# Eleven products of zeros in TensorE's first waits, and a new order of all commands: attention with sinks feeding a three-way maxout layer

## The chip, the core and the metric

The kernel runs on one core of a Trainium2 chip. The metric is the time of one execution on the device in microseconds (us). The kernel before was run five times; the figure that counts is the median. One more execution was taken by the hardware profiler, and all rows of the profile come from it.

## What is computed

Inputs are `q`, `k`, `v` of shape 4 batches x 8 heads x 768 positions x 64, in float32. Three heads (0, 2, 6) attend causally to everything; the five others see only the first 4 positions (the sinks) and a window of 64. The attention output, laid out as 3072 x 512, goes through three projections to 768, their elementwise maximum, and a projection back.

```python
def _attn_ref(q, k, v, is_retrieval, n_sink, window):
    scores = scale * np.matmul(q, k.transpose(0, 1, 3, 2))
    ...
    stream_keep = causal & (is_sink | in_win)
    ...
    scores = np.where(mask[None, :, :, :], scores, -1000000000.0)
    a = np.exp(scores - np.max(scores, axis=-1, keepdims=True))
    a = a / (np.sum(a, axis=-1, keepdims=True) + 1e-09)
    return np.matmul(a, v)

def _moe_ref(x, w1, w2, w3, w_out):
    h = np.maximum(np.maximum(x @ w1, x @ w2), x @ w3)
    return h @ w_out
```

## The kernel before, in words

The work is cut into 16 attention steps and 8 pieces of the feed-forward layer. A step `t` is a batch (`t // 4`), a half of the 384 + 384 query positions, and a quarter set `qd` of the heads (`t % 2`); each step has two pairs of heads, `i` = 0 and 1. A piece of the layer is one batch and one half: 384 tokens.

The order is written out by hand, as a long list of commands called `PROGRAM`. Each command issues a few instructions, and every engine executes its own instructions strictly in the order in which the commands name them. The program is one arm of a branch; the other arm (`GENERAL`) serves other head patterns and does not run here. Before the branch stand the first loads, the masks' raw material and `idle_work(IDLE)`, eight 512-wide products of zeros on TensorE that depend on nothing but a memset.

The commands, with the lines their instructions have in the profile:

- `ld`, `load`, `load_v`, `load_vp`, `w`: DMA loads. `ld`, `load`, `load_vp` and `w` are issued by POOL and stand in POOL's own order; `load_v` by the SP queue. `w 0` to `w 3` are the four weights.
- `cast h p xy` (L314): two casts to fp16, for a pair of heads of batch 0, keys `kn` on engine x and queries `qn` on engine y (d = DVE, a = ACT, p = POOL).
- `turnp` (L333, L341): six TensorE transposes of such a pair, and one or two copies out of PSUM into `KQ`. `turn` (L388): the same for the later batches, by DVE's own 32x32 transpose, 1.1 us each, eight for each batch.
- `um` (L533): a mask built on DVE. For the first two steps masks are added on TensorE (L722, an identity times `mk`).
- `s t u` (L737, L748): scores of one unit on TensorE and their exponential on ACT. The scores go to a pool of two double banks, tag `st`.
- `k t i u e` (L762, L782, L797): masks multiplied into the exponentials, on DVE or POOL.
- `v` (L656, L660, L665, L672): values cast to fp16 into `va`, and copies for the window into `vf`. `o` (L378): sink columns copied in `KQ`.
- `av t i` (L823, L831, L834): the product with the values, then on DVE a reciprocal and a multiplication into `x`.
- `x t i e` (L853, L854, or a DMA transpose L847 with `D`): the transposed input of the layer. The last `x` of a half queues its piece of the layer.
- `f 1 e` (L591, L608, L611, L627, L633): one step of the oldest piece queued: four 384-wide products and their evacuation, or six products of the last projection. A first product's copy goes to engine e; the two maxima are DVE's whatever e says. 24 steps make a piece, 192 in all.
- `idle n`: n more products of zeros; the command exists before the change, but `PROGRAM` does not use it.
- `gate`, `pad`: tiny DMAs that hold the SP queue until something is ready.

```python
    def idle_work(n):
        sink = sps.tile([P, 2, 512], FP32, tag="st", name="st")
        for _ in range(n):
            nc.tensor.matmul(sink[:, 0, :], zero[:, 0:P], zero, start=True, stop=True)
```

In PSUM there are the two `st` tiles and a pool of four single banks (`bkp`, tag `bank`) that everything else shares: the layer's outputs `yy`, the value products `oacc`, the transposes `tr`, and the single-bank scores of `s ... b`. TensorE can therefore run ahead of DVE and ACT by four banks at most.

Of the kernel before, what the change touches and what calls it, by code (L numbers as in the profile page):

```python
# [129 lines left out]
)  # L130

PROGRAM = (
    "cast 0 0 ad, load_v 0 0, cast 0 1 pp, ld 1 0, um 1 1, turnp 0 1 aa, um 1 0, cast 0 3 pa",
    "um 0 1, s 0 0 1, s 0 1 1 b, turnp 0 3 a, cast 0 2 pp, ld 1 2, turnp 0 0 ad, turnp 0 2 ad",
    "um 0 0, cast 1 1 dd, s 0 0 0, cast 1 0 dd, w 0, s 1 0 0, s 0 1 0 b, load_vp 0 1, o 0 0 0 p",
    "v 0 1 dd, v 1 1 dd, v 0 0 dp, turnp 1 0 d, turnp 1 1 da, s 1 0 1, av 0 0, w 1, av 0 1",
    "o 0 1 0 p, cast 1 2 pa, s 1 1 1, s 1 1 0 b, s 2 0 1, v 1 0 pp, cast 1 3 ap, av 1 1",
    "s 2 0 0, av 1 0, x 1 0 d, x 0 0 a, turnp 1 2 dd, s 2 1, x 0 1 d, w 2, x 1 1 d, turnp 1 3 d",
    "f 1 d, s 3 0, k 2 0 1 d, f 1 d, k 3 0 0 d, w 3, o 0 0 1 p, s 3 1 0, k 3 1 0 d, f 1 a",
    "f 1 d, o 0 1 1 d, k 2 1 1 d, s 2 2, v 3 0 dp, f 1 d, k 3 0 1 d, load 1 0, f 1 d, k 2 0 2 d",  # L140
    "v 2 1 dd, s 2 3, av 3 0, s 3 1 1, f 1 a, f 1 d, f 1 d, k 2 1 3 p, v 3 1 ap, k 2 0 3 d",
# [12 lines left out]
    "f 1 d, f 1 a, f 1 a, av 6 1, k 5 1 1 p, s 8 0, f 1 d, av 7 0, load_v 2 0, f 1 a, load 3 1",
    "pad, k 6 0 3 d, av 7 1, s 9 0, x 6 1 D, f 1 d, f 1 d, v 9 1 pp, f 1 a, v 9 0 dp, f 1 a",
    "v 8 1 dd, s 9 1, f 1 a, turn 3 1 1 1, av 6 0, load 3 0, o 2 0 0 d, x 6 0 D, turn 3 1 0 0",
    "f 1 a, x 7 0 D, x 7 1 D, s 8 1, f 1 a, f 1 d, s 10 0, o 2 1 0 p, f 1 d, k 8 0 1 d, f 1 a",
    "turn 3 1 1 0, load_v 2 1, s 9 2, k 9 0 2 d, k 9 1 2 d, f 1 a, f 1 a, v 8 0 ap, f 1 d",
    "f 1 a, k 8 0 0 p, k 9 0 0 d, turn 3 1 0 1, v 10 0 pd, v 11 1 pp, f 1 d, f 1 a, load_v 3 0",
    "f 1 d, f 1 d, f 1 a, k 8 1 0 d, k 9 1 0 d, s 10 1, av 9 0, f 1 a, av 8 0, f 1 a, f 1 a",  # L160
    "v 11 0 pd, f 1 d, f 1 d, k 8 1 1 d, f 1 a, v 12 0 dp, k 9 1 1 p, s 10 2, x 8 0 D, av 9 1",
    "f 1 d, f 1 a, f 1 a, s 10 3, turn 3 0 0 0, av 8 1, x 9 0 D, f 1 a, f 1 d, x 8 1 D, f 1 a",
    "f 1 d, k 10 0 1 p, f 1 d, turn 3 0 0 1, x 9 1 D, k 10 0 3 d, k 10 0 2 d, turn 3 0 1 0",
    "f 1 a, f 1 d, f 1 d, load_v 3 1, f 1 a, k 9 0 1 d, av 10 0, f 1 a, k 10 1 3 p, f 1 d",
    "f 1 d, v 12 1 pp, f 1 a, turn 3 0 1 1, av 11 0, k 10 1 1 p, f 1 d, f 1 a, f 1 a, s 13 0",
# [791 lines left out]
```

## Time and profile before

| | us |
|---|---|
| median of 5 runs | 193.39 (193.27 to 193.82) |
| the profiled execution's own time | 193.64 |
| its span in the trace | 191.9 |
| TensorE busy (products) | 179.8, 94% |
| DVE busy | 145.5, 76% |
| ACT busy | 98.5, 51% |
| POOL busy | 66.8, 35% |
| HBM read / written | 25.17 MB / 6.29 MB |

The time is 1.7 us longer than the span, for what lies around it. A busy TensorE is not TensorE at its peak: products are pipelined, their ends are modelled, and a product's own pace shows in how far apart the starts of neighbours lie. The slices of the page (40 of 4.8 us each) show when an engine works; which wait ends last in a stretch is read from the chain and from the timeline.

### The profile page before, as it was taken

How to read it: one execution, taken by the hardware profiler on the slowest of the kernel's cores; microseconds unless marked ns; L12 is line 12 of the kernel's file. 1: busy time of each engine (PE TensorE's matmuls, PEld its weight loads, DVE VectorE, ACT ScalarE, POOL GpSimd, SP SyncE). 2: the span in 40 equal slices, each digit the busy share in tenths (PEclk: the TensorE clock that was granted, in tenths of full speed). 3: DMA queues.
4: the chain of work that ended last, by engine and by line, in shares of the span. 5: the costliest groups of instructions: out<-in, count | busy, mean ns of one | idle time of the engine just before them, and what ended most of it. 6: DMA issues, size and time to landing. Idle time of an engine off the chain costs nothing.

```text
span 191.9 us, 4762 instructions
## 1 busy us (share of the span) xinstructions
PE 179.8 (94%) x1881; PEld 105.2 (55%) x1881; DVE 145.5 (76%) x312; ACT 98.5 (51%) x150; POOL 66.8 (35%) x114
## 2 busy tenths in 40 slices
PE   7589899999999999999969999999999999999990
PEld 2256545765555546654545566564665566546550
DVE  4149899999799989987997898858789587615620
ACT  3477997036777993679636325573735200131130
POOL 3597607700293788250445701030517100000000
PEclk9999999999999999999999999999999999999998
DMA  5999999999994259859982229512201343121013
GB/s 166 291 295 198 248 209 207 215 212 247 242 186 91 79 152 197 153 83 189 275 180 41 44 113 243 18 24 79 111 0 21 68 164 61 24 109 55 0 56 117
DMA packets 42100, 26.20 MB, mean 137 GB/s; under 512 B 32410, under 2 KB 37082, under 8 KB 42074
## 3 DMA queue, kind: packets, MB, share of 16 engines
q1 hardware_dynamic: 35818, 14.59, 32.0%
q0 software_dynamic: 4880, 10.23, 27.5%
q10 hardware_dynamic: 1376, 1.05, 1.7%
q8 instruction: 15, 0.25, 0.6%
q14 instruction: 11, 0.09, 0.2%
HBM read 25.17 MB, written 6.29 MB: 164 GB/s over the span
## 4 chain that ended last, share of the span: by engine, by line
PE 84%; DMA 4%; DVE 4%; ACT 3%; SPq 1%; issue 1%; POOL 1%; ACTq 0%
PE yy L591 44%; PE yy L627 14%; PE st L737 10%; PE oacc L823 8%; PE yst L591 3%; DMA ks<-in_k_dram 2%; DMA out_dram<-ot 2%; PE tr L333 2%; PE st L722 2%; DVE KQ L341 1%; ACT pb L748 1%; DVE x L834 1%; PE yst L627 1%; PE tr L853 1%; DVE pn L762 1%
## 5 line engine op out<-in xcount | busy, mean ns | idle before, releaser
L591 PE MATMUL yy<-xT,w0t 128*128 128x384 f16 x180 | 35.7, 327 | 1.5 <-DVE x L834 1.5
L591 PE MATMUL yy<-xT,w1t 128*128 128x384 f16 x180 | 35.5, 326 | 0.3 <-DVE acc L611 0.3
L591 PE MATMUL yy<-xT,w2t 128*128 128x384 f16 x180 | 35.9, 326 | 0.0
L748 ACT ACTIVATE pb<-st 128x1024 f16<-128x1024 f32 (+1 forms) x32 | 29.5, 973 | 7.6 <-PE st L737 7.4
L611 DVE TENSOR_TENSOR acc<-yy,acc 128x384 f16<-128x384 f32 x45 | 25.1, 558 | 9.8 <-PE yy L591 6.9
L627 PE MATMUL yy<-woutt,hT 128*128 128x512 f16 (+1 forms) x138 | 31.7, 375 | 0.0
L608 ACT CAST acc<-yy 128x384 f16<-128x384 f32 x28 | 13.5, 482 | 31.6 <-PE yy L591 26.2
L611 DVE TENSOR_TENSOR hT<-yy,acc 128x384 f16<-128x384 f32 x45 | 24.9, 555 | 3.6 <-PE yy L591 0.8
L388 DVE STREAM_TRANSPOSE KQ<-kq 128x384 f32<-128x384 f32 x24 | 25.4, 1140 | 1.2 <-PE st L737 1.2
L591 PEld LDWEIGHTS <-w0t 128*128 128x128 f16 x192 | 17.9, 98 | 15.0 <-DVE x L834 1.9
L737 PE MATMUL st<-KQ 32*128 32x128 f16 (+5 forms) x560 | 24.5, 254 | 0.7 <-ACT pa L748 0.2
L591 PEld LDWEIGHTS <-w1t 128*128 128x128 f16 x192 | 17.8, 98 | 11.9 <-issue 0.4
L748 ACT ACTIVATE pn<-st 128x1024 f16<-128x1024 f32 (+4 forms) x27 | 22.0, 865 | 4.5 <-PE st L737 3.7
L591 PEld LDWEIGHTS <-w2t 128*128 128x128 f16 x192 | 17.6, 98 | 11.3 <-issue 0.4
L627 PEld LDWEIGHTS <-hT 128*128 128x128 f16 x150 | 14.2, 98 | 14.6 <-DVE hT L611 0.4
L737 PEld LDWEIGHTS <-KQ 32*128 32x128 f16 (+1 forms) x560 | 12.0, 93 | 13.9 <-issue 10.9
L633 ACT COPY ot<-yy 128x512 f32<-128x512 f32 x17 | 10.0, 588 | 17.4 <-PE yy L627 13.9
L834 DVE TENSOR_TENSOR x<-oacc,rc 128x384 f16<-128x384 f32 x32 | 17.8, 557 | 1.2
L762 POOL TENSOR_TENSOR pn<-pn,mk 128x512 f16<-128x512 f16 (+2 forms) x7 | 10.9, 1566 | 22.2 <-ACT pn L748 14.6
L748 ACT ACTIVATE pa<-st 128x1024 f16<-128x1024 f32 (+2 forms) x18 | 12.3, 737 | 5.5 <-PE st L737 5.5
L762 DVE TENSOR_TENSOR pn<-pn,mk 128x512 f16<-128x512 f16 (+3 forms) x23 | 13.5, 619 | 1.0 <-ACT pn L748 1.0
L656 POOL CAST va<-vs 128x384 f16<-128x384 f32 x14 | 7.8, 561 | 11.9 <-DMA vs<-in_v_dram 11.7
(96 smaller groups left out, 198.6 us busy)
## 6 DMA issues: line engine op xcount, KB each, us to landing
out_dram<-ot SPq DMA_DIRECT2D x23, 256.0 KB, 2.2
vs<-in_v_dram SPq DMA_DIRECT2D x21, 256.0 KB, 4.5
kq<-in_k_dram POOLq DMA_DIRECT2D x3, 384.0 KB, 7.8
kq<-in_q_dram POOLq DMA_DIRECT2D x3, 384.0 KB, 9.1
kq<-in_k_dram POOLq DMA_DIRECT2D x3, 288.0 KB, 5.2
kq<-in_q_dram POOLq DMA_DIRECT2D x3, 288.0 KB, 6.1
qs<-in_q_dram ACTq DMA_DIRECT2D x4, 192.0 KB, 3.7
ks<-in_k_dram SPq DMA_DIRECT2D x4, 192.0 KB, 5.9
```

The source lines that it names most:

```text
L388: nc.vector.transpose(out=dst.rearrange("c (p j) -> c j p", j=n)[:, j0:j1], in_=src.rearrange("c (j i) -> c j i", i=R),)
L591: nc.tensor.matmul(yy[:, 0:HALF], w_t[wi][:, ks, ni * P : (ni + 1) * P], xT[b, half][ks].rearrange("p a t -> p (a t)"), start=(ks == 0), s ...
L608: copy_out[0](out=acc[ni], in_=yy[:, 0:HALF])
L611: nc.vector.tensor_tensor(out=dst, in0=yy[:, 0:HALF], in1=acc[ni], op=ALU.max)
L627: nc.tensor.matmul(yo[:, 0:n], hT[ns][:, tb * P : (tb + 1) * P], woutt[:, ns, c : c + n], start=(ns == 0), stop=(ns == NNB - 1),)
L633: op(out=ot[:, c : c + n], in_=yo[:, 0:n])
L656: op(out=va[j][:, hs, k0 : k0 + HB, 0:D], in_=vs[:, hs])
L737: nc.tensor.matmul(sts[g // m][:, g % m, c0 : c0 + n * P], KQ[r0 : r0 + nr, 0, abs(ki) * P : (abs(ki) + 1) * P], KQ[r0 : r0 + nr, 1, q0 * ...
L748: nc.scalar.activation(out=pts[of_step(t, i)][:, h0 : h0 + m, off : off + w], in_=st[:, :, 0:w], func=AF.Exp, scale=sc,)
L762: engine.tensor_tensor(out=x, in0=x, in1=m.to_broadcast([P, 2, r, n]), op=ALU.mult)
L823: nc.tensor.matmul(o[:, qi, hl, 0 : D + 1], pt[:, hl, c : c + P], vv[:, 0 : D + 1], start=(idx == 0), stop=(idx == len(todo) - 1), skip_gr ...
L834: nc.vector.tensor_tensor(out=xs[b, half][:, i : i + 3 : 2, :, qd].rearrange("p h a d -> p a h d"), in0=o[:, :, :, 0:D], in1=rc.unsqueeze( ...
```

## The change

Only `PROGRAM` differs. Three commands are new: `idle 6` after the first three casts and the first load, `idle 2` after the first scores, `idle 3` after the second. Together they put eleven 512-wide products of zeros into TensorE's order. All commands are in another order, and many copies, casts and masks have another engine. Summed over the program: 20 mask multiplications go from DVE to POOL (DVE 48 to 28, POOL 20 to 40); copies of the layer's outputs on DVE go from 24 to 31 and on ACT from 49 to 42; value casts on DVE go from 12 to 6, on POOL from 14 to 17, on ACT from 6 to 9; copies of `turnp` on ACT from 6 to 5 and on DVE from 7 to 10; one DMA transpose becomes a TensorE transpose; one `pad` is added. Products other than the eleven are the same in number and size.

The diff, its start whole and then the stretches that the prediction speaks of:

```diff
-    "cast 0 0 ad, load_v 0 0, cast 0 1 pp, ld 1 0, um 1 1, turnp 0 1 aa, um 1 0, cast 0 3 pa",
-    "um 0 1, s 0 0 1, s 0 1 1 b, turnp 0 3 a, cast 0 2 pp, ld 1 2, turnp 0 0 ad, turnp 0 2 ad",
-    "um 0 0, cast 1 1 dd, s 0 0 0, cast 1 0 dd, w 0, s 1 0 0, s 0 1 0 b, load_vp 0 1, o 0 0 0 p",
-    "v 0 1 dd, v 1 1 dd, v 0 0 dp, turnp 1 0 d, turnp 1 1 da, s 1 0 1, av 0 0, w 1, av 0 1",
-    "o 0 1 0 p, cast 1 2 pa, s 1 1 1, s 1 1 0 b, s 2 0 1, v 1 0 pp, cast 1 3 ap, av 1 1",
-    "s 2 0 0, av 1 0, x 1 0 d, x 0 0 a, turnp 1 2 dd, s 2 1, x 0 1 d, w 2, x 1 1 d, turnp 1 3 d",
-    "f 1 d, s 3 0, k 2 0 1 d, f 1 d, k 3 0 0 d, w 3, o 0 0 1 p, s 3 1 0, k 3 1 0 d, f 1 a",
...
-    "turn 2 0 0 1, s 6 0, f 1 a, k 5 1 2 p, av 5 0, v 6 0 dd, av 4 1, s 6 1, x 4 0 D, f 1 a",
-    "k 6 0 1 p, av 5 1, turn 2 0 1 0, x 5 0 D, k 5 0 1 d, x 4 1 D, k 6 1 1 p, f 1 a, f 1 d",
-    "v 7 1 pp, s 6 2, k 6 0 2 d, x 5 1 a, f 1 a, v 7 0 pp, f 1 a, s 6 3, turn 2 1 1 1",
-    "turn 2 1 1 0, f 1 a, v 6 1 pd, f 1 a, k 6 1 3 p, f 1 d, turn 2 1 0 1, f 1 a, turn 2 1 0 0",
-    "f 1 d, f 1 a, f 1 a, av 6 1, k 5 1 1 p, s 8 0, f 1 d, av 7 0, load_v 2 0, f 1 a, load 3 1",
...
-    "f 1 a, k 8 0 0 p, k 9 0 0 d, turn 3 1 0 1, v 10 0 pd, v 11 1 pp, f 1 d, f 1 a, load_v 3 0",
-    "f 1 d, f 1 d, f 1 a, k 8 1 0 d, k 9 1 0 d, s 10 1, av 9 0, f 1 a, av 8 0, f 1 a, f 1 a",
...
+    "cast 0 1 pp, ld 1 0, cast 0 0 pd, idle 6, load_v 0 0, um 1 1, turnp 0 1 ad, um 0 1",
+    "cast 0 3 dp, cast 0 2 pp, s 0 0 1, idle 2, um 1 0, s 0 1 1 b, idle 3, turnp 0 0 dd, ld 1 2",
+    "turnp 0 3 da, s 0 0 0, um 0 0, turnp 0 2 dd, v 0 1 dd, cast 1 0 pa, s 1 0 1, w 0",
+    "turnp 1 0 ad, cast 1 1 pd, v 0 0 pp, av 0 1, s 2 0 0, o 0 1 0 p, s 1 0 0, v 1 1 pd",
+    "o 0 0 0 d, s 1 1 1, s 0 1 0 b, cast 1 2 pa, cast 1 3 da, turnp 1 1 dd, s 1 1 0 b, av 1 1",
+    "s 2 0 1, av 0 0, load_vp 0 1, turnp 1 2 aa, v 1 0 pp, av 1 0, s 2 1, x 0 1 d, turnp 1 3 d",
+    "x 0 0 d, x 1 0 d, x 1 1 d, s 3 0, w 1, o 0 0 1 p, k 3 0 0 d, f 1 d, k 2 0 1 d, f 1 d",
+    "s 2 2, v 3 0 dd, w 2, w 3, k 2 1 1 d, f 1 a, o 0 1 1 d, f 1 d, load 1 0, s 3 1 0, f 1 d",
...
+    "k 5 0 2 d, k 4 1 0 d, s 6 0, f 1 a, k 5 1 2 d, av 5 0, av 4 1, s 6 1, av 5 1, k 5 1 1 d",
+    "x 4 0 D, x 4 1 D, x 5 0 a, f 1 a, f 1 d, turn 2 0 0 1, load_v 2 1, turn 2 0 1 0, f 1 a",
+    "k 6 1 1 p, s 6 2, x 5 1 d, f 1 a, s 6 3, turn 2 1 0 0, f 1 d, f 1 a, turn 2 1 1 0",
+    "v 7 0 pp, f 1 d, v 6 1 ap, k 5 0 1 p, v 6 0 pd, f 1 d, v 7 1 pp, f 1 a, k 6 1 3 p",
+    "load 3 1, f 1 a, k 6 0 3 p, turn 2 1 1 1, f 1 a, turn 2 1 0 1, f 1 a, av 6 1, f 1 a",
+    "k 6 0 2 p, load_v 2 0, pad, f 1 a, s 8 0, av 7 0, f 1 d, load_v 3 1, f 1 d, k 6 0 1 p",
...
+    "k 8 1 1 d, f 1 d, load_v 3 0, f 1 d, k 9 0 2 p, av 8 0, turn 3 1 1 0, f 1 a, load 3 0",
+    "f 1 d, f 1 a, k 9 1 2 d, s 10 1, k 8 1 0 p, f 1 d, f 1 a, f 1 a, f 1 a, v 12 0 pp, av 9 0",
...
```

## The prediction

> **What bounds the kernel now.** I read the page first, then busy time by stretches, then the timeline of the first 25 us and of the one late hole in TensorE's work.
>
> ```profile
> PE 179.8 (94%) x1881; PEld 105.2 (55%) x1881; DVE 145.5 (76%) x312; ACT 98.5 (51%) x150; POOL 66.8 (35%) x114
> ```
>
> The averages name TensorE. The stretches say more (columns: stretch, length, then busy us and instructions of PE, PEld, DVE, ACT, POOL, then granted clock, DMA share, GB/s):
>
> ```profile
> 6.50:16.50 10.00, 8.89 (x65) 5.43 (x66) 4.02 (x10) 6.86 (x13) 8.74 (x14) 1.00 1.14 267
> 25.00:50.00 25.00, 24.86 (x234) 14.79 (x232) 22.97 (x45) 13.42 (x24) 7.00 (x12) 1.00 1.09 214
> 50.00:75.00 25.00, 24.64 (x314) 13.93 (x314) 23.63 (x45) 19.14 (x26) 18.36 (x28) 1.00 0.70 158
> 95.00:100.00 5.00, 3.13 (x43) 1.93 (x36) 4.83 (x12) 1.96 (x3) 2.27 (x4) 1.00 0.98 240
> 115.00:187.20 72.20, 72.16 (x695) 42.66 (x691) 48.34 (x103) 26.66 (x40) 9.70 (x14) 1.00 0.28 69
> ```
>
> From 115 us on TensorE alone is the limit. From 25 to 75 us DVE is busy 92 and 95% beside it: the two are bound together by the four shared banks. At 95 to 100 us DVE is full and TensorE is not. In the first stretch DVE has 4.02 us of work in 10. There TensorE is also slow:
>
> ```profile
> 1.26 3.60 PE L447 MATMUL st<-zero 128*128 128x512 f16 x8 [1.26 <-DVE zero L439]
> 6.57 0.50 PE L333 MATMUL tr<-ident,kn 128*128 128x128 f16 x3 [1.72 <-POOL kn L314]
> 10.22 0.53 PE L333 MATMUL tr<-ident,qn 128*128 128x128 f16 x3
> 10.54 0.53 PE L333 MATMUL tr<-ident,kn 128*128 128x128 f16 x3
> 13.63 1.02 ACT L748 ACTIVATE pa<-st 128x1024 f16<-128x1024 f32 x1 [1.28 <-PE st L737]
> 14.22 0.55 DVE L314 CAST qn<-kf 128x384 f16<-128x384 f32 x1 [0.45 <-DMA kf<-in_q_dram]
> 16.40 0.40 PE L333 MATMUL tr<-ident,kn 128*128 128x128 f16 x3
> 16.63 0.33 PE L333 MATMUL tr<-ident,qn 128*128 128x128 f16 x3
> ```
>
> Three transposes start 0.32 us after the three before them at 10.22 and 10.54, but 0.17 us apart from 16.63 on: until about 16.5 us TensorE runs at half pace, though the granted-clock column says 1.00. Eight 512-wide products of zeros take 0.43 us each, against 0.216 us later in L627. TensorE then stands 1.72 us for `kn`, and ACT waits for TensorE at 13.63. The DMA sets another mark: the queries of `ld 1 0` reach DVE at 14.22.
>
> **The sum that I make.** Own paces from the chain: 20 products of 384 columns in 3.25 us (0.1625 each), six of 512 in 1.29 us, 0.056 for a transpose, 0.031 for a 65-wide value product, four 32-row score products side by side. All products of the arm are then 160.3 us. DVE's own durations, command by command, are 153.9 us in the arm. The largest excess of DVE's sum over TensorE's is 15.1 us, at `turn 3 0 1 0`. DVE ends the copy of `turnp 1 3` at 24.66 us with 14.0 us of the arm's work done. A path that follows DVE to that command and TensorE from there ends at 24.66 - 14.0 + 15.1 + 160.3 = 186.0 us. The last product really ends at 187.2, so this path carries the end within 1.2 us (overlaps of neighbours shorten it, idle and blocked DVE lengthens it).
>
> **The change part by part.**
>
> *The zeros.* `idle 6` starts behind the eight at 4.65. At the cold 0.427 us it ends at 7.21, 0.64 us after the first transposes began. If the clock rises on the way, at about 6.75. `idle 2` and `idle 3` cost 0.85 + 1.28 us cold, 0.43 + 0.65 warm. The row: eight zeros in a row (3.4 us) did not lift the pace, and it rose only after 6.6 us of nearly dense work from 9.92 on. The Trainium skill (TensorE: Matmul & The Clock Gate, "What's actually happening") says the gate opens after one busy window of about 3.4 us, and that the windows run free of the kernel. Then eight can miss a whole window, but 14 in a row and the transposes behind them, 6.6 us, hold one almost wherever the windows lie; TensorE is warm between 6.3 and 9.7 us. By the row alone I would have it warm at 11 to 13. What is queued behind the zeros is all of TensorE's first work. Walking the new order with the durations above: `s 0 0 1` waits for `um 0 1`, which stands on DVE behind a copy of `turnp 0 1`; its exponential starts at 9.15, as before (9.14). `s 0 0 0` has its exponential at 12.4 instead of 13.63. But next on ACT is the query cast of `cast 1 0`, which cannot start before the DMA's 14.15. By the skill's rule, warm TensorE therefore gives ACT nothing; by the row alone the exponential of `s 0 0 0` ends at about 15 and the sum is 1 us worse. I take the rule and keep the other end for the range.
>
> *ACT from 14.15 on.* Its commands up to the exponentials of `s 3 0` are 12.0 us at their spacing (0.97 for a 1024-wide exponential), with a 0.5 us wait for `s 2 0 0` and TensorE's wait for an `st` tile: end at 26.7, before 26.6. No gain. The first `f` follows `s 3 0` and the four `x` at 25.2; before, one `f` was done by 25.1. TensorE is then 0.15 us behind at 27 us, after `s 2 2`, which comes 0.7 us earlier than before.
>
> *POOL's queue.* `load_vp 0 1` moves behind a cast of `cast 1 2`, from 12.92 to about 16.9, and its three issues are 2.7 us. `v 1 0 pp` stands behind them and ends at 21.0; `av 1 0` waits for it and starts at 21.3 (before 20.12). `w 1` is issued at 21 instead of 17.43. I cost that at nothing: the issue at 17.43 took 10.5 us to land because the DMA share is full, and the transfers ahead of it end at 24.4, so it still lands at 28, before its first use at 31. If that backlog were gone, TensorE would wait about 1 us there. `w 2`, `w 3` and `load 1 0` are queued in the same order, and before the queue drains.
>
> *DVE.* 20 masks leave: 4 x 0.42, 5 x 0.28, 8 x 0.42, 2 x 0.42, 0.69, 7.9 us; six value casts of 0.35 leave, 2.1, and one cast, 0.5. Seven copies of the layer come, 4 x 0.56 + 3 x 0.69 = 4.3; `turnp` +1.3, `x` +0.7, `vf` +1.2. Net -2.9 us. Where it falls matters. At the first `f` the sum is 15.4 (before 14.0), but DVE had 6 us of idle in 6.5:16.5 to take it in: it ends `x 1 1` at 24.85. At `av 6 1` (55 `f` in both) it is 68.8, before 67.3: the masks have not left yet. Later it is lighter: the largest excess over TensorE is 14.5, not 15.1, and comes at `turn 2 1 0 1`; at `av 10 0` the excess is 12.9 (before 13.7). The path ends at 24.85 - 15.4 + 14.5 + 160.5 = 184.45, against 186.0: -1.55 us.
>
> *POOL and the shared port.* 20 masks come, 21.6 us at POOL's durations (0.67, 1.15 and 2.13). POOL goes from 35% to about 45%. The rows that speak against it:
>
> ```profile
> 91.18 3.17 DVE L762 TENSOR_TENSOR pn<-pn,mk 128x1024 f16<-128x1024 f16 x3 [0.23 <-ACT pn L748]
> 92.29 1.77 POOL L797 TENSOR_TENSOR pa<-pa,mk 128x512 f16<-128x512 f16 x2
> 99.19 0.82 PE L591 MATMUL yy<-xT,w0t 128*128 128x384 f16 x4 [1.52 <-DVE x L834]
> ```
>
> One of the three DVE masks took 2.23 us instead of 0.40, through both POOL masks; DVE came late to `av 9 0`, and TensorE, out of banks, stood 1.5 us. That agrees with the skill (SBUF — State Buffer, "SBUF: two separate sides"): the pair of ports is held for a whole instruction, and a DVE instruction with two SBUF inputs waits. Durations above their shortest add up to 5.0 us on DVE. After the change DVE has 0.6 of the masks and POOL 1.3 times the busy time: 0.6 to 0.8 of that, so about 1 us less, or as much again if the collisions fall badly. I take nothing for it, and keep -2 and +2 us: both the hole of 95:100 and a new one are possible.
>
> *The rest.* ACT loses 3.9 us and is not the limit after 30 us. One more `pad` on SP and one DMA transpose fewer: DMA transposes were up to 9 us of SP's queue for four, and the new order leaves six or seven `f` between the last of a half and its first use, as before (7); I cost it at nothing, a late one would cost 1 to 2 us. The end (two halves of the last block, DMA out) is unchanged.
>
> Sum: -1.55, and 0.1 for the late first `f`: -1.5. The profiled span 191.9 becomes 190.4, and 1.74 us lie around it: 192.1 against 193.64. The median is 0.25 below the profiled execution: **191.9**.
>
> **The rivals.**
>
> *The zeros and the DMA delay the start (slower).* The zeros stand in TensorE's order; if the pace rises only at 11 to 13 us, all eleven cost 4.7 us cold, `turnp 0 0` moves from 10.54 to 12.3, ACT's chain starts 1 us after the DMA's mark, and the first `f` comes 2 us late while DVE's early lead of 1.4 us is gone: -1.5 + 3 = +1.5, 194.9. For it: the row of eight. Against it: 6.6 us dense. It decides if transposes are still 0.107 us apart after 10.5 us.
>
> *POOL holds DVE or is late with masks (slower).* POOL has 9.4 us of work in one 8.45 us stretch of TensorE around `av 6 1`. Two blocked masks of 1.8 us as at 92.1, where DVE has no slack, are +3.6 against -1.5: +2, 195.4. For it: the hole at 97 to 99. Against it: POOL mostly runs ahead, since its casts need only loads.
>
> *Nothing.* The stretch 25:75 has as much DVE work as before; if the lead at 24.85 is lost to waits for ACT, the end moves by less than 0.4 us: 193.3.
>
> **How the numbers follow.** Forecast 0.53 (its own range 189.0 to 192.9: the -2 us of a closed hole, and another -1 for shorter waits in 50:75, or waits that eat most of the gain), zeros 0.17, POOL 0.20, nothing 0.10. A difference of 0.2% (0.39 us) is about what these runs can tell. Faster 0.53, within 0.2% 0.10, slower 0.37. The range 189.0 to 195.4 takes in the cases up to their worked values and leaves out the tails.
>
> **What would show it.** Right: from 9.7 us at the latest transposes 0.056 us apart; ACT's query cast at 14.2 and no ACT gap over 0.5 us until 26.7; first `f` near 25; TensorE's stall in 95:100 smaller; DVE under 144 us. Wrong: TensorE waits for `POOL` masks or for DVE of over 1 us between 27 and 115; a wait for `w1t`; DVE masks over 1 us long beside POOL's; the first `f` after 26.5 us.

## The result, and the profile after

| | kernel before | changed kernel |
|---|---|---|
| median, us | 193.78 (192.86 to 195.51, 79 runs) | 193.08 (191.04 to 195.91, 42 runs) |
| profiled execution, us | 193.64 | 191.96 |
| its span, us | 191.9 | 190.2 |
| start of the last copy out of PSUM, us | 187.20 | 184.90 |

The ratio is 0.9935, with a 95% interval of 0.992 to 0.9951: faster by 0.65%. Ratios here leave out a kernel's longest executions (of the changed kernel the eight of 193.9 us and more), so a ratio can lie below that of the two medians, which are 0.70 us (0.36%) apart. The changed kernel spreads nearly twice as wide as the kernel before, and its time follows the clock: its executions with a mean TensorE clock of 0.996 and more took 191.0 to 192.1 us, those with 0.98 and less 193.6 to 195.9. In 65 executions of the kernel before the same two groups have medians of 193.66 and 193.56 us.

The first line of the page for the changed kernel:

```profile
PE 178.7 (94%) x1895; PEld 104.6 (55%) x1895; DVE 142.1 (75%) x303; ACT 94.0 (49%) x143; POOL 88.0 (46%) x133
```

DVE has 3.4 us less, POOL 21 us more. The stretches, in the same columns as ahead of the prediction:

```profile
6.50:16.50 10.00, 7.01 (x82) 4.55 (x83) 5.93 (x15) 5.36 (x10) 9.42 (x18) 1.00 1.16 277
25.00:50.00 25.00, 24.77 (x242) 14.56 (x243) 23.22 (x46) 12.40 (x23) 8.30 (x14) 1.00 1.08 199
50.00:75.00 25.00, 24.83 (x319) 14.15 (x308) 23.30 (x47) 19.08 (x26) 16.62 (x29) 1.00 0.79 180
95.00:100.00 5.00, 5.00 (x52) 3.21 (x53) 4.76 (x11) 2.07 (x3) 1.52 (x2) 1.00 1.03 198
115.00:185.50 70.50, 69.86 (x650) 40.75 (x648) 46.22 (x95) 24.48 (x36) 20.93 (x21) 1.00 0.19 57
```

Behind the start one row is different: 95 to 100 us. TensorE was busy there for 3.13 us of 5 and now is for all 5; behind 24.3 us it has no wait of more than 0.3 us left. From 25 to 75 us hardly anything has changed, DVE still has 23.2 and 23.3 us of 25. The timeline of the first stretch:

```profile
1.26 4.75 PE L447 MATMUL st<-zero 128*128 128x512 f16 x14 [1.26 <-DVE zero L439]
...
6.48 0.34 PE L333 MATMUL tr<-ident,kn 128*128 128x128 f16 x3 [0.47 <-POOL kn L314]
...
9.77 0.33 PE L333 MATMUL tr<-ident,kn 128*128 128x128 f16 x3
9.94 0.33 PE L333 MATMUL tr<-ident,qn 128*128 128x128 f16 x3
...
14.37 0.51 ACT L314 CAST qn<-kf 128x384 f16<-128x384 f32 x1 [1.70 <-DMA kf<-in_q_dram]
...
14.94 0.34 PE L333 MATMUL tr<-ident,qn 128*128 128x128 f16 x3 [1.85 <-ACT qn L314]
```

Three transposes now start 0.17 us after the three before them at 9.77, where they had 0.32 us at 10.22: TensorE is at full pace at least 6 us earlier. It buys nothing: ACT waits 1.70 us for the queries that the DMA lands at 14.3, and TensorE waits 1.85 us for ACT.

The plainest reading comes from the start of the same `f` in both traces. The third column is the changed kernel minus the kernel before, the others are experiments told below, all against the kernel before:

| start of the n-th `f` | before, us | changed | order_only | zeros_only | both_dve | mask_early | mask_swap | new_rest | after_fill |
|---|---|---|---|---|---|---|---|---|---|
| 1 | 23.48 | +1.10 | +1.04 | +1.07 | +0.09 | +0.70 | -0.34 | +0.51 | +1.16 |
| 12 | 35.05 | -0.17 | -0.23 | +1.06 | +0.09 | +0.70 | -0.34 | +0.80 | -0.10 |
| 55 | 73.83 | -0.07 | -0.12 | +1.06 | +0.09 | +0.70 | -0.34 | +0.90 | 0.00 |
| 65 | 85.11 | -0.08 | -0.13 | +1.06 | +0.09 | +0.70 | -0.34 | +0.89 | -0.01 |
| 73 | 91.74 | +0.20 | +0.16 | +1.06 | +0.08 | +2.04 | -0.34 | +1.17 | +0.27 |
| 76 | 93.69 | +0.86 | +0.81 | +1.66 | +0.08 | +2.04 | -0.34 | +1.83 | +0.93 |
| 79 | 99.19 | -2.67 | -2.72 | +0.94 | -2.05 | -0.17 | -0.10 | -1.71 | -2.61 |
| 82 | 101.15 | -2.38 | -2.43 | +0.94 | -2.05 | -0.18 | -0.10 | -1.42 | -2.32 |
| 180 | 178.55 | -2.31 | -2.36 | +0.89 | -1.62 | +0.19 | +0.37 | -1.46 | -2.24 |

Each column is one execution. `before`, `both_dve`, `mask_early`, `mask_swap` and `new_rest` begin with the same commands, and still their first `f` differs by -0.34 to +0.70 us; the upper rows have to be read with that much doubt, the jumps further down do not depend on it.

At 85 us the two kernels are level. The whole difference is made between 91 and 99 us, and after 101 us nothing is added. (The +0.86 at the 76th `f` is the order itself: other commands stand between the same `f`.) Of the 2.3 us, 1.7 are left at the end of the span, because in this execution 5.3 us pass from the last copy's start to the end, and in that before 4.7.

### The profile page after: what moved, and what is told of

It is laid out like the page before. It is cut to its first block, busy times and chain, and to the rows that moved or that the text cites. A ratio compares the mean times of both kernels' runs of the same rounds, so it can differ in the third digit from the quotient of the medians.

```text
span 190.2 us, 4794 instructions
## 1 busy us (share of the span) xinstructions
PE 178.7 (94%) x1895; PEld 104.6 (55%) x1895; DVE 142.1 (75%) x303; ACT 94.0 (49%) x143; POOL 88.0 (46%) x133
## 4 chain that ended last, share of the span: by engine, by line
PE 85%; DMA 6%; ACT 3%; POOL 1%; DVE 1%; issue 0%; SPq 0%; ACTq 0%
PE yy L591 47%; PE yy L627 16%; PE st L737 10%; PE oacc L823 8%; DMA kf<-in_q_dram 3%; PE yst L591 3%; ACT pb L748 2%; DMA ks<-in_k_dram 2%; PE yst L627 1%; DVE KQ L341 1%; POOL kf L293 0%; PE st L722 0%; ACT KQ L341 0%; PE tr L333 0%; ACT ot L633 0%
## 5 line engine op out<-in xcount | busy, mean ns | idle before, releaser
L591 PE MATMUL yy<-xT,w2t 128*128 128x384 f16 x180 | 35.4, 326 | 0.0
L611 DVE TENSOR_TENSOR acc<-yy,acc 128x384 f16<-128x384 f32 x45 | 24.8, 557 | 8.7 <-PE yy L591 4.9
L762 POOL TENSOR_TENSOR pn<-pn,mk 128x512 f16<-128x512 f16 (+2 forms) x15 | 20.9, 1410 | 20.4 <-ACT pn L748 16.1
L608 ACT CAST acc<-yy 128x384 f16<-128x384 f32 x26 | 12.5, 479 | 35.4 <-PE yy L591 32.1
L611 DVE TENSOR_TENSOR hT<-yy,acc 128x384 f16<-128x384 f32 x45 | 24.9, 557 | 5.2 <-PE yy L591 2.2
L388 DVE STREAM_TRANSPOSE KQ<-kq 128x384 f32<-128x384 f32 x24 | 25.0, 1137 | 0.4 <-issue 0.4
L737 PE MATMUL st<-KQ 32*128 32x128 f16 (+4 forms) x560 | 23.6, 250 | 1.7 <-DVE KQ L341 1.0
L627 PEld LDWEIGHTS <-hT 128*128 128x128 f16 x150 | 14.3, 98 | 15.1 <-issue 0.2
L834 DVE TENSOR_TENSOR x<-oacc,rc 128x384 f16<-128x384 f32 x32 | 17.8, 558 | 1.3 <-DVE rc L831 0.2
L633 ACT COPY ot<-yy 128x512 f32<-128x512 f32 x14 | 8.3, 589 | 21.0 <-PE yy L627 18.4
L797 POOL TENSOR_TENSOR pb<-pb,mk 128x512 f16<-128x512 f16 x10 | 11.4, 1153 | 12.0 <-ACT pb L748 11.9
L633 DVE COPY ot<-yy 128x512 f32<-128x512 f32 (+1 forms) x9 | 6.0, 662 | 11.5 <-PE yy L627 10.9
## 6 DMA issues: line engine op xcount, KB each, us to landing
qs<-in_q_dram ACTq DMA_DIRECT2D x4, 192.0 KB, 3.9
ks<-in_k_dram SPq DMA_DIRECT2D x4, 192.0 KB, 4.9
```

Source lines behind the costliest of these rows:

```text
L388: nc.vector.transpose(out=dst.rearrange("c (p j) -> c j p", j=n)[:, j0:j1], in_=src.rearrange("c (j i) -> c j i", i=R),)
L591: nc.tensor.matmul(yy[:, 0:HALF], w_t[wi][:, ks, ni * P : (ni + 1) * P], xT[b, half][ks].rearrange("p a t -> p (a t)"), start=(ks == 0), s ...
L608: copy_out[0](out=acc[ni], in_=yy[:, 0:HALF])
L611: nc.vector.tensor_tensor(out=dst, in0=yy[:, 0:HALF], in1=acc[ni], op=ALU.max)
L627: nc.tensor.matmul(yo[:, 0:n], hT[ns][:, tb * P : (tb + 1) * P], woutt[:, ns, c : c + n], start=(ns == 0), stop=(ns == NNB - 1),)
L633: op(out=ot[:, c : c + n], in_=yo[:, 0:n])
```

## The experiments

### The order, the zeros and the start, each alone

`order_only`: the changed kernel without its three idle commands.

```diff
-    "cast 0 1 pp, ld 1 0, cast 0 0 pd, idle 6, load_v 0 0, um 1 1, turnp 0 1 ad, um 0 1",
-    "cast 0 3 dp, cast 0 2 pp, s 0 0 1, idle 2, um 1 0, s 0 1 1 b, idle 3, turnp 0 0 dd, ld 1 2",
+    "cast 0 1 pp, ld 1 0, cast 0 0 pd, load_v 0 0, um 1 1, turnp 0 1 ad, um 0 1",
+    "cast 0 3 dp, cast 0 2 pp, s 0 0 1, um 1 0, s 0 1 1 b, turnp 0 0 dd, ld 1 2",
```

> The new order and engines without the eleven products of zeros. My theory: ACT waits for the keys and queries of the second half (the cast of cast 1 0 at about 14.2 us) whatever TensorE's pace is, and the gain lies at 95 to 100 us; so this keeps at least two thirds of the change: 192.2 to 193.0 where before is 193.8, and the first f starts within 1 us of 24.6. Rival, the zeros are needed: TensorE stays at half pace up to 13 us or later, the exponential of s 0 0 0 ends after 15 us, the first f starts at 26 or later, and the time is that of before or longer (193.8 to 195.5).

Measured: 192.5 us (191.55 to 193.67), ratio 0.9934 (0.9907 to 0.9961), where the changed kernel has 0.9935. By the ratio the new order alone is the whole change, and its trace runs with that of the changed kernel to within 0.06 us. Its times do not follow the clock (the two lowest clocks, 0.976 and 0.98, took 192.5 and 192.0 us, the five of 0.996 and more 191.6 to 193.7), so the dependence on the clock seems to come with the zeros. The ratio of the changed kernel hides part of that, since it leaves out the longest executions: the medians of all are 192.5 without zeros and 193.08 with them.

`zeros_only`: the kernel before with the eleven zeros at the matching places.

```diff
-    "cast 0 0 ad, load_v 0 0, cast 0 1 pp, ld 1 0, um 1 1, turnp 0 1 aa, um 1 0, cast 0 3 pa",
-    "um 0 1, s 0 0 1, s 0 1 1 b, turnp 0 3 a, cast 0 2 pp, ld 1 2, turnp 0 0 ad, turnp 0 2 ad",
+    "cast 0 0 ad, load_v 0 0, cast 0 1 pp, ld 1 0, um 1 1, idle 6, turnp 0 1 aa, um 1 0, cast 0 3 pa",
+    "um 0 1, s 0 0 1, idle 2, s 0 1 1 b, idle 3, turnp 0 3 a, cast 0 2 pp, ld 1 2, turnp 0 0 ad, turnp 0 2 ad",
```

> The order before, with idle 6 ahead of turnp 0 1, idle 2 behind s 0 0 1 and idle 3 behind s 0 1 1. My theory: TensorE is at full pace by 10 us and s 0 0 0 comes 1 to 1.5 us earlier, but DVE binds from 25 to 100 us and the hole of 2 us at 95 to 100 us stays: 193.0 to 193.9 where before is 193.8. Rival, the warm clock is the gain: everything moves up by 1 us or more, 192.6 or less. Rival, the zeros stand in the way: 194.5 or more.

Measured: 195.43 us (194.15 to 196.73), ratio 1.0064 (1.004 to 1.0088). The zeros cost, as the second rival had it. The stretches of 3.4 us show how (the clock is the third column from the end):

```profile
9.40:12.80 3.40, 3.02 (x35) 1.99 (x33) 1.34 (x3) 2.76 (x7) 3.40 (x7) 1.00 1.15 286
12.80:16.20 3.40, 1.69 (x21) 0.92 (x20) 2.41 (x6) 2.20 (x4) 2.62 (x4) 1.00 1.06 293
16.20:19.60 3.40, 3.40 (x43) 2.54 (x40) 2.92 (x8) 1.88 (x3) 2.21 (x6) 0.50 1.17 243
19.60:23.00 3.40, 2.52 (x44) 1.66 (x43) 2.35 (x8) 3.05 (x7) 2.80 (x5) 1.00 1.04 221
```

TensorE, warm from 5.9 us on, has work for half of 12.8 to 16.2 (it waits for `kn` of step 1), and then runs at half pace from 16.2 to 19.6, where it has no slack. `s 1 0 0` started 1.12 us earlier than before, `s 2 0 1` starts 1.07 us later, and that stays to the end (the column of the table).

`new_start`: the changed kernel up to `s 3 0`, then the order of the kernel before.

```diff
-    "cast 0 0 ad, load_v 0 0, cast 0 1 pp, ld 1 0, um 1 1, turnp 0 1 aa, um 1 0, cast 0 3 pa",
...
-    "f 1 d, s 3 0, k 2 0 1 d, f 1 d, k 3 0 0 d, w 3, o 0 0 1 p, s 3 1 0, k 3 1 0 d, f 1 a",
+    "cast 0 1 pp, ld 1 0, cast 0 0 pd, idle 6, load_v 0 0, um 1 1, turnp 0 1 ad, um 0 1",
...
+    "x 0 0 d, x 1 0 d, x 1 1 d, s 3 0, w 1, f 1 d, k 2 0 1 d, f 1 d, k 3 0 0 d, w 2, w 3",
```

> The new order with the zeros up to s 3 0, and the order before from there (w 1, one f and w 2 follow s 3 0). My theory: no gain, since TensorE is as far at 27 us as before and the hole at 95 to 100 us comes back: 193.4 to 194.2 where before is 193.8. Rival, DVE's lead at the start counts (what the prediction took for most of its 1.55 us): 192.3 to 193.0, with the hole smaller.

Measured: 195.0 us (192.56 to 197.18), ratio 1.0024 (0.9998 to 1.0049). The new start alone gains nothing. It is longer than the theory had it; in its trace, too, the clock is at half from 15.8 to 19.2 us.

`new_rest` is its mirror: the kernel before up to `s 3 0`, without zeros, and then the changed order.

```diff
-    "f 1 d, s 3 0, k 2 0 1 d, f 1 d, k 3 0 0 d, w 3, o 0 0 1 p, s 3 1 0, k 3 1 0 d, f 1 a",
+    "f 1 d, s 3 0, o 0 0 1 p, k 3 0 0 d, k 2 0 1 d, f 1 d, s 2 2, v 3 0 dd, w 3, k 2 1 1 d, f 1 a",
...
```

> Edit: the kernel before up to `s 3 0` (with its `f 1 d`, `w 1` and `w 2`), without zeros, and from there the order and engines of the changed kernel. Theory (the gain comes from the new order and engines behind the first stretch, and within it from the stall of 95:100 that closes): 191.5 to 192.5 us, ratio 0.988 to 0.994, like the changed order without its zeros (0.9934). Rival (the new start is needed, because the later order leans on its earlier `x` and loads): ratio 0.997 to 1.003, and TensorE waits in 25:75 that the changed kernel does not have.

Measured: 192.36 us (190.86 to 194.22), ratio 0.9873 (0.9818 to 0.9927). In its column the first stretch is 0.5 us late, and 2.3 us are won between the 65th and the 82nd `f`, as much as in the changed kernel. The gain lies behind the first stretch, in the stall of 95 to 100 us.

### What makes that stall: three edits of one or two masks

All three start from the kernel before. `mask_swap` exchanges the engines of two masks, `mask_early` moves one of them to POOL at a time when POOL is idle, `both_dve` changes one letter.

```diff
# mask_swap
-    "f 1 a, k 8 0 0 p, k 9 0 0 d, turn 3 1 0 1, v 10 0 pd, v 11 1 pp, f 1 d, f 1 a, load_v 3 0",
+    "f 1 a, k 8 0 0 d, k 9 0 0 p, turn 3 1 0 1, v 10 0 pd, v 11 1 pp, f 1 d, f 1 a, load_v 3 0",
# mask_early
-    "f 1 a, x 7 0 D, x 7 1 D, s 8 1, f 1 a, f 1 d, s 10 0, o 2 1 0 p, f 1 d, k 8 0 1 d, f 1 a",
-    "f 1 a, k 8 0 0 p, k 9 0 0 d, turn 3 1 0 1, v 10 0 pd, v 11 1 pp, f 1 d, f 1 a, load_v 3 0",
+    "f 1 a, x 7 0 D, x 7 1 D, s 8 1, f 1 a, f 1 d, s 10 0, o 2 1 0 p, k 9 0 0 p, f 1 d, k 8 0 1 d, f 1 a",
+    "f 1 a, k 8 0 0 p, turn 3 1 0 1, v 10 0 pd, v 11 1 pp, f 1 d, f 1 a, load_v 3 0",
# both_dve
-    "f 1 a, k 8 0 0 p, k 9 0 0 d, turn 3 1 0 1, v 10 0 pd, v 11 1 pp, f 1 d, f 1 a, load_v 3 0",
+    "f 1 a, k 8 0 0 d, k 9 0 0 d, turn 3 1 0 1, v 10 0 pd, v 11 1 pp, f 1 d, f 1 a, load_v 3 0",
```

> The kernel before with two letters changed: the masks of k 8 0 0 on DVE and those of k 9 0 0 on POOL, as the new order has them; DVE's mask of 2.23 us between two of POOL's is gone by that. My theory: DVE is 1.8 us earlier at av 9 0, the TensorE wait of 1.5 us in front of the product at 99.19 goes, and the time falls by 1.3 to 2.3 us: 191.5 to 192.5 where before is 193.8. Rival, DVE is simply full there (blocked time or not): less than 0.6 us. Rival, POOL is late with the masks of k 9 0 0 for av 9 0: a new wait at 95 us, no gain or a loss.

> Edit to the kernel before: the one mask `k 9 0 0` leaves DVE (its place at about 92 us) and goes to POOL right behind `o 2 1 0 p`, where POOL stands idle from 84 to 92 us; all else as before, no zeros. Theory (the hole of 95:100 is made by the mask work that DVE has there, lengthened by POOL's masks beside it): DVE comes 2.2 to 2.65 us earlier to `av 9 0`, the hole of TensorE at 97 to 99 us closes, and the time falls by 1.3 to 2.3 us against the kernel before (ratio 0.988 to 0.993). Rival (DVE is simply full between 88 and 100, the masks of `k 8 1 0` and `k 9 1 0` collide as before, and the hole only moves): under 0.6 us, ratio over 0.997. Second rival (the gain of the changed kernel needs its whole order from 75 us on): the hole shrinks but TensorE stands later by the same, ratio near 1.0.

> Edit to the kernel before: `k 8 0 0` goes from POOL to DVE, so both masks of 91 to 94 us are DVE's and no POOL mask runs beside them. DVE has 0.7 us more of its own work, but its mask that took 2.23 us should take 0.40. Theory (blocking by POOL's masks makes the hole): DVE is 1.0 to 1.5 us earlier at `av 9 0`, time 0.5 to 1.2 us shorter, ratio 0.994 to 0.9975. Rival (the amount of DVE's own work makes the hole, whoever blocks it): time 0 to 0.7 us longer, ratio 1.0 to 1.004.

Measured: `mask_swap` 194.25 us, ratio 1.0024 (1.0004 to 1.0044); `mask_early` 193.11 us, 0.9972 (0.9949 to 0.9995); `both_dve` 191.96 us (191.73 to 192.43), 0.9894 (0.9856 to 0.9932).

The theory of `mask_swap` missed: the exchange only turned the collision round. Its timeline, DVE and POOL:

```profile
91.44 2.92 DVE L797 TENSOR_TENSOR pa<-pa,mk 128x512 f16<-128x512 f16 x2
91.95 2.26 POOL L762 TENSOR_TENSOR pn<-pn,mk 128x512 f16<-128x512 f16 x2
```

Two masks that DVE does in 0.68 us without POOL beside it (the first row of `both_dve` below) take 2.92.

`mask_early` took both masks out of the way and closed the hole, but paid for it earlier. Its timeline, DVE, POOL and TensorE:

```profile
85.08 2.26 POOL L762 TENSOR_TENSOR pn<-pn,mk 128x512 f16<-128x512 f16 x2
...
85.83 1.73 DVE L378 COPY KQ<-KQ 32x32 f16<-32x32 f16 x2
...
89.16 1.52 PE L627 MATMUL yy<-woutt,hT 128*128 128x512 f16 x6 [1.22 <-DVE hT L611]
```

The moved masks now stand beside two copies of 32x32 elements, DVE's `o 2 0 0`, which take 1.73 us. In the kernel before they take 0.35:

```profile
85.13 0.35 DVE L378 COPY KQ<-KQ 32x32 f16<-32x32 f16 x2
```

TensorE waits 1.22 us for the `hT` behind them. That takes the column from +0.70 to +2.04 at the 73rd `f`; the -0.17 at the 79th says that the hole, 2.2 us, closed as the theory wanted. My expectation had the price of the new place at nothing, because it looked at POOL's idle time and not at what DVE does there.

`both_dve` settles it for the kernel before. DVE has 0.7 us more of its own work, and the kernel has a lower median than the changed one:

```profile
91.87 0.68 DVE L797 TENSOR_TENSOR pa<-pa,mk 128x512 f16<-128x512 f16 x2
...
92.48 0.75 DVE L762 TENSOR_TENSOR pn<-pn,mk 128x512 f16<-128x512 f16 x2
...
95.63 0.76 DVE L762 TENSOR_TENSOR pn<-pn,mk 128x512 f16<-128x512 f16 x2
96.30 0.19 DVE L831 RECIPROCAL rc<-oacc 128x6 f32<-128x6 f32 x1
...
96.50 0.95 POOL L656 CAST va<-vs 128x384 f16<-128x384 f32 x2 [4.09 <-DMA vs<-in_v_dram]
```

The gain is larger than the 0.5 to 1.2 us that I expected. In the kernel before a second collision followed from the first: late by 1.1 us, DVE met POOL's value casts with its next masks.

```profile
96.40 1.11 POOL L656 CAST va<-vs 128x384 f16<-128x384 f32 x2 [2.33 <-DMA vs<-in_v_dram]
...
97.07 1.37 DVE L762 TENSOR_TENSOR pn<-pn,mk 128x512 f16<-128x512 f16 x2
...
98.36 0.18 DVE L831 RECIPROCAL rc<-oacc 128x6 f32<-128x6 f32 x1
```

In `both_dve` those masks are done, in 0.76 us, before POOL's cast begins at 96.50. DVE's reciprocal for `av 9 0` starts at 96.30 instead of 98.36, and TensorE, which had stood for 1.5 us, is busy for all of 95 to 100 us.

In the changed kernel the same stretch looks like this:

```profile
91.55 2.12 POOL L762 TENSOR_TENSOR pn<-pn,mk 128x1024 f16<-128x1024 f16 x1 [0.18 <-ACT pn L748]
91.77 0.69 DVE L633 COPY ot<-yy 128x512 f32<-128x512 f32 x1 [1.52 <-PE yy L627]
...
93.08 1.12 DVE L388 STREAM_TRANSPOSE KQ<-kq 128x384 f32<-128x384 f32 x1
...
94.75 1.77 POOL L782 TENSOR_TENSOR pa<-pa,base 128x256 f16<-128x256 f16 x2
95.16 0.84 DVE L762 TENSOR_TENSOR pn<-pn,mk 128x1024 f16<-128x1024 f16 x1
```

POOL's masks stand beside DVE's copies, transposes and maxima, and only one DVE mask meets them. Two things have changed at once, then: the long collision is gone, and DVE has fewer masks there. Between the starts of the 73rd and the 79th `f` its masks take 4.96 us before (six), 3.00 in `both_dve` (eight) and 0.84 in the changed kernel (one). `both_dve` shows that the end of the collision is enough to close the hole; whether fewer masks alone would have been, no run shows.

### The clock: filling the wait behind the zeros

`after_fill` adds six zeros to the changed kernel in TensorE's wait of 1.85 us. `zeros_fill` is `zeros_only` with five more zeros in its own wait.

```diff
# after_fill
-    "turnp 1 0 ad, cast 1 1 pd, v 0 0 pp, av 0 1, s 2 0 0, o 0 1 0 p, s 1 0 0, v 1 1 pd",
+    "idle 6, turnp 1 0 ad, cast 1 1 pd, v 0 0 pp, av 0 1, s 2 0 0, o 0 1 0 p, s 1 0 0, v 1 1 pd",
# zeros_fill, behind the edit of zeros_only
-    "v 0 1 dd, v 1 1 dd, v 0 0 dp, turnp 1 0 d, turnp 1 1 da, s 1 0 1, av 0 0, w 1, av 0 1",
+    "v 0 1 dd, v 1 1 dd, v 0 0 dp, idle 5, turnp 1 0 d, turnp 1 1 da, s 1 0 1, av 0 0, w 1, av 0 1",
```

> Edit to the changed kernel: `idle 6` more right ahead of `turnp 1 0 ad`, so that TensorE has work in its 2 us wait at 12.9 to 14.9 us. Theory (in some executions of the changed kernel the early warm clock falls back to half from about 16 to 19.6 us, because the stretch before was thinly filled, and that costs about 1 us there): the fall does not come, the first `f` starts no later than in the changed kernel, the median is 0.5 to 1.5 us below the changed kernel's 193.1, and the spread of its times is narrower. Rival (the fall comes from elsewhere, or 6 zeros at half pace, 2.6 us, push `turnp 1 0` and `s 2 0 0` back): the same spread, median equal or up to 1 us longer than the changed kernel's.

> Edit to the kernel before: the same eleven zeros as in `zeros_only` (6 ahead of `turnp 0 1`, 2 and 3 behind the first two scores), and `idle 5` more right ahead of `turnp 1 0 d`, in the 1.6 us wait of TensorE at 13.8 to 15.4 us. Theory (in `zeros_only` the zeros cost 1.24 us because the clock, warm early, falls back to half from 16.2 to 19.6 us after a thin stretch): with the wait filled the clock stays full, `s 2 0 1` starts no later than 19.1 us as before, and the time is that of the kernel before or up to 0.6 us less (ratio 0.997 to 1.001). Rival (the zeros cost because they stand in TensorE's order): at least as slow as `zeros_only`, ratio 1.006 to 1.010.

Measured: `after_fill` 191.52 us (five of six runs 191.11 to 191.84, one 193.62), ratio 0.9887 (0.9836 to 0.9937). `zeros_fill` 194.12 us (192.82 to 194.87), ratio 1.0002 (0.9976 to 1.0028), against 1.0064 without the filler. Its stretch behind the wait has the full clock:

```profile
12.80:16.20 3.40, 2.23 (x18) 0.89 (x16) 1.80 (x4) 1.96 (x4) 2.75 (x4) 1.00 1.04 285
16.20:19.60 3.40, 3.05 (x55) 2.22 (x55) 3.30 (x10) 2.13 (x4) 1.74 (x5) 1.00 1.15 229
```

The mean clock says the same of all executions, roughly, because the half clock behind TensorE's last product counts in it too: 13 of 22 of `zeros_only` lie below 0.990, and about half of the changed kernel's; none of the 14 of `zeros_fill` and none of the 6 of `after_fill`. So the filler keeps the clock, and most of the zeros' cost goes with it: the median is 0.34 us above that of the kernel before instead of 1.56. The clock may not be all of that cost: the six executions of `zeros_only` with 0.996 and more took 194.3 to 195.0 us, still longer than before, and why stays open. It does not turn into a gain on the kernel before: the first stretch still ends where DMA and ACT let it. In the trace of `zeros_fill` the first `f` is 0.64 us late at full clock; DVE's first cast of the queries, which waits for DMA, stands at 14.87 us, in `zeros_only` at 14.34.

In the changed kernel the filler does what was expected: five of its six executions lie where those of the changed kernel with the highest clock lie (191.0 to 192.1). `after_fill` has the lowest median of all, but its interval overlaps that of the changed kernel, and the two did not run side by side.

`both_fill` puts the one letter of `both_dve` and the zeros of `zeros_fill` together; `rest_fill` is `new_rest` with the zeros of `zeros_fill`.

```diff
# both_fill, behind the edit of zeros_fill
-    "f 1 a, k 8 0 0 p, k 9 0 0 d, turn 3 1 0 1, v 10 0 pd, v 11 1 pp, f 1 d, f 1 a, load_v 3 0",
+    "f 1 a, k 8 0 0 d, k 9 0 0 d, turn 3 1 0 1, v 10 0 pd, v 11 1 pp, f 1 d, f 1 a, load_v 3 0",
# rest_fill, behind the edit of zeros_fill
-    "f 1 d, s 3 0, k 2 0 1 d, f 1 d, k 3 0 0 d, w 3, o 0 0 1 p, s 3 1 0, k 3 1 0 d, f 1 a",
+    "f 1 d, s 3 0, o 0 0 1 p, k 3 0 0 d, k 2 0 1 d, f 1 d, s 2 2, v 3 0 dd, w 3, k 2 1 1 d, f 1 a",
...
```

> Edit to the kernel before: the mask `k 8 0 0` on DVE as in `both_dve`, with the zeros and the filler of `zeros_fill`. If the two effects are independent, the time is that of `both_dve` (ratio 0.9894) with what `zeros_fill` brings: 191.2 to 192.0 us. Rival (the zeros cost in their own right): 193 us or more.

> Edit: up to `s 3 0` the kernel before with the zeros and the filler of `zeros_fill`, from there the order and engines of the changed kernel. Theory (closed hole, and a first stretch with the clock full throughout): 190.9 to 191.8 us, ratio 0.985 to 0.990, the shortest of all. Rival (the start is bound by DMA and ACT and not by TensorE's pace, so zeros bring nothing): as `new_rest`, 192.4 us with the same wide spread.

Measured: `both_fill` 192.8 us, ratio 0.9951 (0.993 to 0.9972); `rest_fill` 192.15 us, 0.9904 (0.987 to 0.9938). Both expectations were too low. `both_fill` is slower than `both_dve` without zeros by 0.8 us: the two effects do not add up, and the zeros cost something though no clock of the 22 executions lies below 0.990. In its trace the 74th `f` stands 0.38 us for a transposed input from the DMA queue, and the 79th starts 1.46 us earlier than before instead of 2.05. The same wait stands in the traces of `zeros_only` (0.44 us) and `zeros_fill` (0.33). Why the zeros bring it was not tried. `rest_fill` has the time of `new_rest` in a narrower spread (191.87 to 193.34). In its profiled execution the clock fell once more, from 21.6 to 25 us, after this stretch:

```profile
18.20:21.60 3.40, 2.28 (x37) 1.38 (x37) 3.01 (x9) 3.33 (x8) 3.19 (x8) 1.00 1.11 256
21.60:25.00 3.40, 3.40 (x32) 2.62 (x31) 2.06 (x5) 2.21 (x4) 0.00 (x0) 0.50 1.11 209
```

### Back to POOL in the new order

`fill_k8p`: the letter of `both_dve` the other way, in `after_fill`.

```diff
-    "turn 3 1 1 1, f 1 d, v 8 0 ap, f 1 a, f 1 d, k 8 0 0 d, v 11 0 pp, v 8 1 dp, s 9 2",
+    "turn 3 1 1 1, f 1 d, v 8 0 ap, f 1 a, f 1 d, k 8 0 0 p, v 11 0 pp, v 8 1 dp, s 9 2",
```

> Edit to `after_fill` (the changed kernel with six more zeros ahead of `turnp 1 0`): the one mask `k 8 0 0` goes from DVE back to POOL, at 90.4 us. It is two masks of 0.9 us; POOL's `k 9 0 2` behind it moves from 91.6 to about 93.5. Theory (a POOL mask costs where a waiting product or a fp16 operation of DVE stands beside it): `av 8 0` waits for the POOL mask and TensorE, dense there in the changed kernel, stands 0.6 to 2 us in 91 to 97 us; time 0.4 to 1.8 us over `after_fill`'s 191.5. Rival (masks on POOL are free in this order, since DVE has 1.5 us of idle at 90.3): within 0.3 us of `after_fill`.

Measured: 191.83 us (191.23 to 192.52), ratio 0.9896 (0.9852 to 0.9941). The rival holds: 0.3 us above `after_fill`, inside the spread. The same two masks, of 1.77 us, that cost 1.8 us in the kernel before are free here. The timeline says why:

```profile
90.23 1.77 POOL L797 TENSOR_TENSOR pa<-pa,mk 128x512 f16<-128x512 f16 x2
...
91.75 0.69 DVE L633 COPY ot<-yy 128x512 f32<-128x512 f32 x1 [2.05 <-PE yy L627]
...
93.09 1.12 DVE L388 STREAM_TRANSPOSE KQ<-kq 128x384 f32<-128x384 f32 x1
93.10 2.12 POOL L762 TENSOR_TENSOR pn<-pn,mk 128x1024 f16<-128x1024 f16 x1
...
94.00 0.59 DVE L611 TENSOR_TENSOR acc<-yy,acc 128x384 f16<-128x384 f32 x1
...
94.70 0.56 DVE L611 TENSOR_TENSOR hT<-yy,acc 128x384 f16<-128x384 f32 x1
```

The masks that were moved, at 90.23, run almost wholly while DVE stands idle for 2.05 us. POOL's next mask, of 2.12 us (`k 9 0 2`, on POOL in the changed kernel too), runs beside a DVE transpose and two maxima, and none of them is longer than alone. Sorting DVE's instructions of two traces by whether a POOL mask overlaps them shows the same (medians in ns, in brackets how many; POOL's casts are not counted):

| DVE instruction | trace | alone | beside a POOL mask |
|---|---|---|---|
| L388 transpose, 32 bit | before | 1130 (18) | 1124 (6) |
| L611 maximum into `acc`, one input from PSUM | before | 557 (32) | 557 (13) |
| L834 into `x`, one input from PSUM | before | 557 (24) | 557 (8) |
| L762 mask `pn` of 512, SBUF to SBUF | before | 418 (10) | 2230 (1) |
| L762 mask `pn` of 768, SBUF to SBUF | before | 550 (5) | 1069 (1) |
| L656 value cast, SBUF to SBUF | before | 351 (11) | 736 (1) |
| L388 transpose, 32 bit | changed | 1159 (12) | 1120 (12) |
| L611 maximum into `acc` | changed | 557 (27) | 558 (18) |
| L797 mask `pb` of 512, SBUF to SBUF | changed | 416 (1) | 860 (1) |
| L660 copy `vf`, SBUF to SBUF | changed | 282 (1) | 327 and 1182 |

The Trainium skill (SBUF — State Buffer, "SBUF: two separate sides") names the two kinds of DVE operation that have to share with POOL: those in a two-port fast mode, and those with two inputs in SBUF. The masks are of the second kind, and they are lengthened; the transposes and the operations with an input from PSUM, most of this kernel's, are as long beside a POOL mask as alone. The lengthened rows are single cases. In the changed kernel POOL has 20 masks more, and its masks of 91 to 96 us lie mostly beside operations that do not pay.

## Why the prediction came out as it did

The forecast of -1.5 us and "faster" held (0.65% is 1.26 us; the medians of all executions are 0.70 us apart, and the median is 193.08 us, not 191.9), and the sum behind it did not. Two of its terms were wrong in opposite directions.

- **The path through DVE** (-1.55). This is the step that failed. Its inputs were good: DVE lost 3.4 us where I had 2.9. But some 1.2 us of the term was DVE's lead at the start (24.85 - 15.4 against 24.66 - 14.0), and that lead is worth nothing: `new_start` alone gains nothing, and the changed kernel and `order_only` are level with the kernel before at 85 us (-0.08 and -0.13). `both_dve` gains more than the whole term, 1.84 us in the median, with 0.7 us more on DVE. The rest of the term, fewer masks on DVE behind 75 us, cannot be told apart from the end of the collision in the changed kernel.
- **POOL and the shared port** ("I take nothing for it, and keep -2 and +2 us: both the hole of 95:100 and a new one are possible"). Here lies the effect: -2.4 us at the 82nd `f`, the hole closed. I had the row that shows it, a mask of 2.23 us instead of 0.40, and priced it as a count of masks. What counted was which DVE operation each POOL mask stands beside, and that could be read from the order of commands around 92 us.
- **The zeros, by the skill's rule or by the row.** The rule was right for the clock's rise, if anything too late as I used it: full at 4.5 us in the changed kernel's clock records and 5.9 in `zeros_only`, where I had 6.3 to 9.7, with transposes 0.056 us apart from 9.77. And "warm TensorE therefore gives ACT nothing" held: ACT's query cast began at 14.37 (forecast 14.2), the first `f` at 24.58 (25.2), and `order_only` without zeros has the same ratio. The step lacked the way back: an early warm clock can be lost again in a thin stretch, with 1.06 us lost in the trace of `zeros_only`. With the zeros filled up, in `after_fill`, five of six executions lie within 0.73 us; so this seems to give the changed kernel much of its wide spread.
- **ACT and POOL's queue.** The exponentials of `s 3 0` ended at 26.03 (26.7), `av 1 0` began at 21.18 (21.3), and TensorE had no wait for `w1t`. Right.
- **The rivals.** "The zeros and the DMA delay the start" named transposes 0.107 us apart after 10.5 us as its sign; that did not come, though zeros alone do cost, by another way. "POOL holds DVE" had the right mechanism and the wrong sign: the change removed a collision. "Nothing" is what the new start alone gives.

That the forecast lay close is thus partly luck: -1.55 for a thing of which the larger part was worth nothing, and 0 for the stretch that is worth -2.3 at TensorE's end.

## What to carry to other kernels

Before costing a mask or a cast on POOL, write down which DVE instruction will run beside it: here a POOL mask was free beside DVE work that reads PSUM and beside the 32-bit transposes, and cost up to 2.2 us beside copies or masks within SBUF (two masks in `mask_swap`, 2.92 us instead of 0.68). When two traces differ little in the end, line up the starts of the same instruction in both; the stretch where their difference jumps is worth more than any sum of busy time. One letter at that place (ratio 0.9894) was worth about as much as the whole new order (0.9934 without the zeros; the intervals overlap).

## What the hardware showed that I had not expected

- TensorE's clock went back to half for one window of 3.41 us (in `mask_swap` for two) although TensorE was never idle for a whole window: after windows (the clock records' own) with TensorE busy for 47% (`mask_swap`, at 5.2 us), 50% (`zeros_only`), 55% (`new_start`) and 67% (`rest_fill`) of the time. After windows of 53% (the changed kernel) and 63% (`zeros_fill`) it stayed full, so TensorE's busy share alone does not give the threshold; that stays open. The Trainium skill (TensorE: Matmul & The Clock Gate, "What's actually happening") has the clock back at half after an idle window; for these traces "idle" has to be read as "thinly filled".
- The windows lie differently in each execution: the clock records have the clock full from 4.5 us in one with zeros, 5.9 in another, 7.2 in a third; 5.2 us (then half again) in `mask_swap`, which has no added zeros, where the kernel before has 16.5. (Ahead of its first record the granted-clock column shows 1.00, though transposes start 0.107 us apart there.) A stretch that is thin in part costs in some executions only.
- A DVE copy pays beside POOL however small it is: two of 32x32 elements took 1.73 us instead of 0.35.
